# One written order for every engine, and PSUM banks shared in four pairs, in an attention and feed-forward kernel

## The chip, the cores and the metric

The kernel runs on one core of a Trainium2 chip. The time is device microseconds (us) of one execution; the number that is compared is the median of several runs. TensorE is called PE, its weight loads PEld, VectorE DVE, ScalarE ACT, GpSimd POOL and SyncE SP, as in the profile.

## What is computed

```python
# q, k, v: (4, 8, 768, 64); n_sink = 4; window = 128
scores = q @ k.T / 8
keep   = (key < 4) | ((0 <= query - key) & (query - key < 128))
a      = softmax(where(keep, scores, -1e9))
x      = (a @ v) with the heads side by side        # (3072, 512)
h      = (x @ w1) * (x @ w2)                        # 1024 wide
out    = (h @ w3) @ w_out                           # (3072, 512)
```

## The kernel before

The work is cut into named units, and each unit has stages on different engines. A unit's first number is mostly the batch b (0 to 3).

- `c`: a weight that SP has loaded raw is cast to bf16, on ACT or DVE. `t3.i.h` (line 588) transposes half of row block i of w3 on PE and copies it out of PSUM; `fm.i.h` (line 618) multiplies it by w_out, two matmuls in each unit, so that `w3 @ w_out` becomes one folded weight `w3o`.
- `tpk.b.kb` (line 295) transposes a block of keys and queries on PE; `td.b.kb` (line 303) does the same for later blocks by a DMA that SP issues. `ko`, `vo`, `sk` and `sv` are small DVE copies that bring sink keys and values beside the window's.
- `sc.b.x.t` are scores (lines 377, 428, 450): PE matmuls that use 64 rows of the array, ACT's exponential, DVE's product with a mask. `ss` are the scores of the sink keys, on 32 rows (line 348). `av.b.x.t` (lines 412, 483, 520) multiplies by the values; DVE then takes a reciprocal and scales.
- `xt` transposes the result on PE, `xd` by a DMA of SP (line 558).
- `g.b.c.dt.half` (line 571) is PE work for one chunk of tokens and one block of w1 (half 0, copied out by ACT at line 578) or w2 (half 1, multiplied by DVE at line 575).
- `p.b.m` (line 632) multiplies by `w3o`; ACT or DVE copies the result out (line 636) and SP stores it (line 641).

PE's order is a written list, `TURNS`. ACT, DVE and SP have no written order: a planner, `plan`, walks through time with a cost for each stage, estimated landing times of the loads (`landings`) and a table of small preferences (`LEAN`), and emits each engine's instructions in the order that results. So every engine's order is fixed when the program is built. Where PE would idle early on, the planner puts in matmuls on zeros (`keep_busy`, line 649).

PSUM has eight banks. The pool `ps_mm` has four one-bank buffers that rotate, for everything but scores; `ps_sc` has two buffers of two banks each, for scores and for the folds 0 to 3.

POOL issues the loads of q, k, v, of w1 and w2 and of part of w3, one after another. For batches 2 and 3 it waits, before each load, until the load four places back has landed (`send_load`).

Of the kernel before, what the change touches and what calls it, by code (L numbers as in the profile page):

```python
# [20 lines left out]
def kernel(  # L22
# [13 lines left out]
    nc = tc.nc  # L36
# [26 lines left out]
    PAIRED = ()  # L63
    BLOCKS = ((0, 0), (0, 1))
    SINKS = (1,)
    PAIRS = (2, 3)
    X_TURNED = ((1, 1), (1, 2)) + tuple((b, u) for b in (2, 3) for u in range(NT))
    HALVED = ((3, 1), (3, 2), (3, 3))
    SPLIT = 6
    OTHER = {("fm", 1, 3), ("fm", 7, 3), ("p", 2, 2), ("p", 2, 3), ("p", 2, 5), ("p", 3, 1), ("p", 3, 2), ("p", 3, 4),  # L70
             ("t3", 0, 1), ("t3", 1, 1), ("t3", 2, 1), ("t3", 3, 1), ("t3", 5, 0), ("t3", 6, 1), ("t3", 7, 1), ("tpk",
             0, 1), ("tpk", 1, 1), ("xt", 0, 0, 0), ("xt", 0, 2, 0), ("xt", 0, 2, 2), ("xt", 1, 0, 0)}
# [5 lines left out]
    work = ctx.enter_context(tc.tile_pool(name="work", bufs=3))  # L78
# [46 lines left out]
    AHEAD = 4  # L125
    sent = []

    def send_load(b, dst, src):

        if b >= 2 and len(sent) >= AHEAD:  # L130
            nc.gpsimd.tensor_copy(spent[:], sent[-AHEAD])  # L131
        nc.gpsimd.dma_start(out=dst, in_=src)  # L132
        sent.append(dst[:, 0, 0:1])

    def of_pair(b, m):

        x = kqN[b][:, 2 * m:2 * m + 2].rearrange("p k i x -> p (k i x)")
        return x.rearrange("p (i h s d) -> p i h s d", i=2, s=2, d=D)

    def load_qk(b, kb):  # L140

        if (b, kb // 2) in PAIRED:
            for i, src in enumerate((k, q)):
                if kb % 2 == 0:
                    send_load(b, of_pair(b, kb // 2)[:, i].rearrange("p h s d -> p h (s d)"),
                              src[b, :, kb * P:kb * P + 256, :].rearrange("h (p s) d -> p h (s d)", s=2))
            return
        for src, dst in ((k, kN), (q, qN)):
            send_load(b, heads(dst[b][:, kb, :]), rows(src, b, kb * P, (kb + 1) * P))

    def load_v(b, kb):

        for s in VSLOTS[kb] if b in LATE else (kb,):
            t0, t1 = KEYS[s] if b in LATE else (kb * P, (kb + 1) * P)
            send_load(b, vN[b][:, s, :, 0:D], rows(v, b, t0, t1))
# [48 lines left out]

    nudge = {}
# [77 lines left out]
    def copy_stage(name, act, act_us, dve_us):  # L283

        return ("act", act_us) if act != (name in OTHER) else ("dve", dve_us)

    def transposes(b, kb):

        tp = ps_mm.tile([P, 2, NP, P], BF16, tag="mm", name="tp")
        m, s = kb // 2, kb % 2  # L290
        paired = (b, m) in PAIRED
        for i, src in enumerate((kN[b], qN[b])):
            for r in range(NP):
                turn = of_pair(b, m)[:, i, 2 * r:2 * r + 2, s, :] if paired else src[:, kb, r * P:(r + 1) * P]
                nc.tensor.transpose(tp[:, i, r, :], turn, ident)  # L295
        yield
        copier(("tpk", b, kb), False)(kqT[b][:, :, :, bass.ds(256 * m + s, P, step=2) if paired else slice(kb * P, (kb + 1) * P)],
                              tp[:])
        yield
# [43 lines left out]
    def sink_scores(b, t0, t1):  # L343

        sp = ps_mm.tile([P, (t1 - t0) * 256], FP32, tag="mm", name="sp")
# [14 lines left out]
    def late_scores(b, r, u):  # L360
# [12 lines left out]
        sc = ps_sc.tile([P, 2, 512], FP32, tag="sc", name="sc")  # L373
# [5 lines left out]
        ex = work.tile([P, 2, 512], BF16, tag="ex", name="ex")  # L379
        nc.scalar.activation(ex[:, :, 0:n], sc[:, :, 0:n], ACTF.Exp, scale=scale)  # L380
        yield
        am = work.tile([P, 2, 512], BF16, tag="am", bufs=4, name="am")
        mv = 2 * min(u, 1)
        nc.vector.tensor_mul(am[:, :, 0:n], ex[:, :, 0:n], maskt[:, mv:mv + 1, 0:n].to_broadcast([P, 2, n]))  # L384
        ams[b, r, u] = am
        yield

    def late_values(b, r, u):
# [3 lines left out]
        av = ps_mm.tile([P, n, 2, D + 1], FP32, tag="mm", name="av")  # L392
# [18 lines left out]
        for x, (o, lhs, rhs) in enumerate(todo):  # L411
            nc.tensor.matmul(o, lhs, rhs, start=(x == 0), stop=(x == len(todo) - 1), skip_group_check=True)  # L412
        yield
        m = P if u == 0 else 112
        rec = work.tile([P, 3, 2, 1], FP32, tag="rec", name="rec")
        nc.vector.reciprocal(rec[0:m, 0:n], av[0:m, :, :, D:D + 1])  # L416
        if (b, u) not in xns:
            xns[b, u] = work.tile([P, n, NP, 2, D], BF16, tag="xn" if u else "xa", bufs=3 if u else 1, name="xn")
# [3 lines left out]
    def scores(b, r, t):  # L422
        c0 = P if t == 0 else 0
        sc = ps_sc.tile([P, 2, 512], FP32, tag="sc", name="sc")
# [7 lines left out]
        ex = work.tile([P, 2, 512], BF16, tag="ex", name="ex")  # L432
        nc.scalar.activation(ex[:, :, c0:], sc[:, :, c0:], ACTF.Exp, scale=scale)
        yield
        am = work.tile([P, 2, 512], BF16, tag="am", bufs=4, name="am")
        m0 = MA if t == 0 else MT
        mk = maskt[:].rearrange("p (o v) x -> p o (v x)", o=1)[:, :, m0:m0 + 512 - c0].to_broadcast([P, 2, 512 - c0])
        nc.vector.tensor_mul(am[:, :, c0:], ex[:, :, c0:], mk)
        ams[b, r, t] = am
        yield  # L440

    def block_scores(b, j, r0, r1):

        kbs = [kb for kb in (j - 1, j) if kb >= 0]
        sc = ps_sc.tile([P, 2, r1 - r0, len(kbs), P], FP32, tag="sc", name="sc")
        for r in range(r0, r1):
            for s, kb in enumerate(kbs):
                for e in range(2):
# [4 lines left out]
        ex = work.tile([P, 2, 512], BF16, tag="ex", name="ex")  # L453
        nc.scalar.activation(ex[:], sc[:].rearrange("p e r s q -> p e (r s q)"), ACTF.Exp, scale=scale)
        yield
        am = work.tile([P, 2, 512], BF16, tag="am", bufs=4, name="am")
# [4 lines left out]
                             .to_broadcast([P, 2 * (r1 - r0), n]))  # L461
        for r in range(r0, r1):
# [3 lines left out]
    xns = {}  # L466

    def block_values(b, j, r0):

        t, i = j // 2, j % 2  # L470
        av = ps_mm.tile([P, 2, 2, D + 1], FP32, tag="mm", name="av")
# [10 lines left out]
        for n, (o, lhs, rhs) in enumerate(todo):  # L482
            nc.tensor.matmul(o, lhs, rhs, start=(n == 0), stop=(n == len(todo) - 1),
                             skip_group_check=True)
        yield
        rec = work.tile([P, 3, 2, 1], FP32, tag="rec", name="rec")[:, 0:2]
        nc.vector.reciprocal(rec, av[:, :, :, D:D + 1])
        if (b, t) not in xns:
            xns[b, t] = work.tile([P, 2, NP, 2, D], BF16, tag="xn", bufs=3, name="xn")
# [4 lines left out]
    def block_x_transposes(b, j):  # L494

        t, i = j // 2, j % 2
        xt = ps_mm.tile([P, NP, P], BF16, tag="mm", name="xt")
        for r in range(NP):
            nc.tensor.transpose(xt[:, r, :], xns[b, t][:, i, r, :, :].rearrange("p e d -> p (e d)"), ident)
        yield  # L500
# [3 lines left out]
    def values(b, r, t):  # L504

        am = ams.pop((b, r, t))
        av = ps_mm.tile([P, 2, 2, D + 1], FP32, tag="mm", name="av")
# [11 lines left out]
        for n, (o, lhs, rhs) in enumerate(todo):  # L519
            nc.tensor.matmul(o, lhs, rhs, start=(n == 0), stop=(n == len(todo) - 1),  # L520
                             skip_group_check=True)
        yield
        rec = work.tile([P, 3, 2, 1], FP32, tag="rec", name="rec")[:, 0:2]
        nc.vector.reciprocal(rec, av[:, :, :, D:D + 1])
        if (b, t) not in xns:
            xns[b, t] = work.tile([P, 2, NP, 2, D], BF16, tag="xn", bufs=3, name="xn")
# [4 lines left out]
    def x_transposes(b, r0, t):  # L531

        xt = ps_mm.tile([P, 2, 2, P], BF16, tag="mm", name="xt")
        for r in range(2):
            for i in range(2):
                nc.tensor.transpose(xt[:, r, i, :],
                                    xns[b, t][:, i, r0 + r, :, :].rearrange("p e d -> p (e d)"),
                                    ident)
        yield
# [4 lines left out]
    def late_x_transposes(b, u, i):  # L544
# [3 lines left out]
        xt = ps_mm.tile([P, NP, m], BF16, tag="mm", name="xt")  # L548
        for r in range(NP):
            nc.tensor.transpose(xt[:, r, :], xns[b, u][0:m, i, r, :, :].rearrange("p e d -> p (e d)"), ident[0:m, 0:m])  # L550
        yield
# [3 lines left out]
    def x_transposes_dma(b, t, i):  # L555
# [3 lines left out]
                                    in_=xns[b, t][0:q1 - q0, i].rearrange("p r e d -> p (r e d)"))  # L559
        yield  # L560
# [3 lines left out]
    def gate(b, c, dt, half):  # L564
# [4 lines left out]
        pg = ps_mm.tile([P, n], FP32, tag="mm", name="pg")  # L569
# [4 lines left out]
        if half:  # L574
            nc.vector.tensor_mul(ab[b][:, dt, tk], gate_a.pop((b, c, dt))[:], pg[:])  # L575
        else:
            a_sb = work.tile([P, n], FP32, tag="a_sb", bufs=4, name="a_sb")
            nc.scalar.copy(a_sb[:], pg[:])  # L578
# [5 lines left out]
    def fold_w3(i, j0, j1):  # L584

        tp = ps_mm.tile([P, j1 - j0, P], BF16, tag="mm", name="tp3")
# [17 lines left out]
    def folded(i):  # L604
        return ("fm", i, len(FM[i]) - 1)

    def fold_mm(i, j0, j1):

        if i >= 4:
            if j0 == 0:  # L610
                held[i] = ps_mm.tile([P, DM], FP32, tag="mm", name="pw")
            po = held[i][:]
        else:
            if i % 2 == 0 and j0 == 0:
                held[i // 2] = ps_sc.tile([P, 2, DM], FP32, tag="sc", name="ph")
# [12 lines left out]
    def project(b, m, n0, n1):  # L628

        po = ps_mm.tile([P, n1 - n0], FP32, tag="mm", name="po")  # L630
# [14 lines left out]
    def keep_busy(n):  # L645

        pz = ps_mm.tile([P, 512], FP32, tag="mm", name="pz")
# [4 lines left out]
    arrive = {}  # L652
    arrive["vc",] = 20.0

    def service(what, *i):
        if what == "qkv":
            return [(0.95 if i[0] == 0 else 0.87, (1.65 if (i[0], s // 2) in PAIRED and x != "v" else 1) * (0.845 if i[0] == 0 else 0.9 if i[0] == 1 else 1.72),
                     [(x, i[0], n) for n in ((s, s + 1) if (i[0], s // 2) in PAIRED and x != "v" else (s,))])
                    for y, kb in pieces(*i)
                    for x, s in ([("k", kb), ("q", kb)] if y == "kq" else  # L660
                                 [("v", s) for s in (VSLOTS[kb] if i[0] in LATE else (kb,))])
                    if (i[0], kb // 2) not in PAIRED or x == "v" or kb % 2 == 0]
        if what == "w3":
            return [(0.75, 1.3 * (i[1] - i[0]), [("w3", x) for x in range(*i)])]
        if what == "wo":
            return [(0.81, 0.65 * (i[1] - i[0]), [("wo", x) for x in range(*i)])]
        return [(0.8, 1.34 * (i[1] - i[0]), [(w,) + (n,) for n in range(i[0], i[1])]) for w in ("w1", "w2")]
# [536 lines left out]
```

## Time and profile before

| | |
|---|---|
| median of 3 runs | 192.89 us (192.27 to 193.19) |
| the profiled execution | 193.17 us, of which its span is 191.5 us |
| PE busy | 184.6 us, 96% of the span |
| DVE, ACT, POOL busy | 125.9, 102.5, 91.5 us |
| PE matmuls at line 571 (gates) and 632 (projection) | 91.5 and 43.0 us busy |
| moved by DMA | 30.02 MB |

A row of the timeline gives start and length in us, engine, line, operation, what is written and read, and how many instructions were merged; in brackets stands the idle time before it with what ended it. Matmuls overlap, so the step between the starts of rows tells what a matmul costs, and its own length tells how long its result takes. In a row of the stretches the numbers behind the stretch are its length and the busy us (with the count of instructions) of PE, PEld, DVE, ACT and POOL. A row of a group ends with busy us, mean ns of one, and the idle us before them. Some records of matmuls are missing from the trace.

### The profile page before, as it was taken

How to read it: one execution, taken by the hardware profiler on the slowest of the kernel's cores; microseconds unless marked ns; L12 is line 12 of the kernel's file. 1: busy time of each engine (PE TensorE's matmuls, PEld its weight loads, DVE VectorE, ACT ScalarE, POOL GpSimd, SP SyncE). 2: the span in 40 equal slices, each digit the busy share in tenths (PEclk: the TensorE clock that was granted, in tenths of full speed). 3: DMA queues.
4: the chain of work that ended last, by engine and by line, in shares of the span. 5: the costliest groups of instructions: out<-in, count | busy, mean ns of one | idle time of the engine just before them, and what ended most of it. 6: DMA issues, size and time to landing. Idle time of an engine off the chain costs nothing.

```text
span 191.5 us, 4799 instructions
## 1 busy us (share of the span) xinstructions
PE 184.6 (96%) x1874; PEld 122.3 (64%) x1893; DVE 125.9 (66%) x302; ACT 102.5 (54%) x171; POOL 91.5 (48%) x149
## 2 busy tenths in 40 slices
PE   7899999999999999999999999999999999999993
PEld 2345557988688776767788876665556675555442
DVE  4554688846688778878896877785888653532320
ACT  3363578643967568756738575464687233230112
POOL 4298977699992468786756667640000000000000
PEclk9999999999999999999999999999999999999999
DMA  6999999999999999999999999999511022000525
GB/s 217 407 377 171 170 159 197 195 163 153 150 179 177 125 188 154 153 144 226 180 180 220 182 160 158 185 181 190 193 29 39 13 67 88 6 0 14 184 94 205
DMA packets 112551, 30.02 MB, mean 157 GB/s; under 512 B 103184, under 2 KB 108432, under 8 KB 112528
## 3 DMA queue, kind: packets, MB, share of 16 engines
q0 software_dynamic: 82640, 12.72, 97.7%
q1 hardware_dynamic: 29744, 16.92, 37.7%
q8 instruction: 15, 0.25, 0.5%
q10 hardware_dynamic: 144, 0.07, 0.1%
q14 instruction: 8, 0.07, 0.1%
HBM read 30.15 MB, written 6.29 MB: 190 GB/s over the span
## 4 chain that ended last, share of the span: by engine, by line
PE 76%; DMA 13%; POOL 6%; issue 1%; SPq 1%; ACT 0%
PE pg L571 42%; PE po L632 21%; DMA w_sb<-in_moe_w_dram 5%; PE av L412 5%; PE sc L377 5%; DMA vN<-in_v_dram 4%; DMA ab<-in_moe_w_out_dram 4%; POOL w_sb L159 3%; POOL kqN L132 2%; PE tp L295 1%; SPq L217 1%; PE av L520 1%; PE sc L428 1%; POOL vN L132 0%; ACT w_sb L636 0%
## 5 line engine op out<-in xcount | busy, mean ns | idle before, releaser
L571 PE MATMUL pg<-xT,w_sb 128*128 128x256 bf16 (+3 forms) x640 | 91.5, 294 | 0.2 <-DMA w_sb<-in_moe_w_dram 0.2
L571 PEld LDWEIGHTS <-w_sb 128*128 128x128 bf16 x640 | 59.4, 98 | 20.7 <-DMA w_sb<-in_moe_w_dram 0.4
L578 ACT COPY a_sb<-pg 128x256 f32<-128x256 f32 (+3 forms) x80 | 32.6, 417 | 34.1 <-PE pg L571 31.9
L575 DVE TENSOR_TENSOR ab<-a_sb,pg 128x256 bf16<-128x256 f32 (+3 forms) x80 | 37.1, 471 | 19.4 <-PE pg L571 18.1
L632 PE MATMUL po<-w3o,ab 128*128 128x512 bf16 (+2 forms) x193 | 43.0, 361 | 0.7
L380 ACT ACTIVATE ex<-sc 128x928 bf16<-128x928 f32 (+1 forms) x36 | 34.4, 972 | 5.0 <-PE sc L377 4.7
L632 PEld LDWEIGHTS <-ab 128*128 128x128 bf16 x208 | 19.3, 98 | 19.3
L636 ACT COPY w_sb<-po 128x512 f32<-128x512 f32 (+2 forms) x19 | 10.6, 558 | 29.9 <-PE po L632 28.1
L132 POOL DMA_DIRECT2D vN<-in_v_dram x27 | 24.2, 905 | 3.4 <-issue 1.8
L384 DVE TENSOR_TENSOR am<-ex,maskt 128x928 bf16<-128x928 bf16 (+1 forms) x36 | 23.1, 651 | 1.2 <-ACT ex L380 1.1
L132 POOL DMA_DIRECT2D kqN<-in_q_dram x24 | 21.8, 909 | 3.9 <-issue 2.8
L132 POOL DMA_DIRECT2D kqN<-in_k_dram x24 | 21.9, 911 | 3.5 <-issue 2.2
L419 DVE TENSOR_TENSOR xn<-av,rec 112x256 bf16<-112x256 f32 (+1 forms) x36 | 16.9, 469 | 1.2
L412 PEld LDWEIGHTS <-am 128*128 128x128 bf16 x312 | 12.9, 98 | 4.0
L416 DVE RECIPROCAL rec<-av 112x4 f32<-112x4 f32 (+1 forms) x36 | 6.6, 183 | 10.9 <-PE av L412 10.6
L412 PE MATMUL av<-vN,am 128*128 128x65 bf16 x216 | 13.7, 193 | 0.0
L636 DVE COPY w_sb<-po 128x512 f32<-128x512 f32 (+1 forms) x7 | 4.3, 633 | 10.5 <-PE po L632 7.3
L131 POOL CAST spent<-kqN 128x1 f32<-128x1 bf16 x24 | 6.3, 264 | 9.5 <-DMA kqN<-in_k_dram 7.1
L377 PE MATMUL sc<-kqT 64*128 64x112 bf16 (+3 forms) x168 | 10.0, 218 | 0.0
L618 PE MATMUL ph<-wo_sb,kown 128*128 128x512 bf16 x31 | 8.5, 380 | 0.7 <-DVE wo_sb L598 0.3
L377 PEld LDWEIGHTS <-kqT 64*128 64x128 bf16 x168 | 6.8, 94 | 3.5 <-issue 3.0
L377 PE MATMUL sc<-kqT,kown 64*128 64x112 bf16 (+2 forms) x120 | 8.7, 208 | 0.0
(94 smaller groups left out, 178.4 us busy)
## 6 DMA issues: line engine op xcount, KB each, us to landing
out_dram<-w_sb SPq DMA_DIRECT2D x20, 256.0 KB
vN<-in_v_dram POOLq DMA_DIRECT2D x27, 128.0 KB, 6.5
kqN<-in_k_dram POOLq DMA_DIRECT2D x24, 128.0 KB, 6.1
kqN<-in_q_dram POOLq DMA_DIRECT2D x24, 128.0 KB, 6.1
w_sb<-in_moe_w_dram POOLq DMA_DIRECT2D x9, 256.0 KB, 8.3
ab<-in_moe_w_dram SPq DMA_DIRECT2D x4, 512.0 KB
ab<-in_moe_w_out_dram SPq DMA_DIRECT2D x2, 512.0 KB
kqN<-in_moe_w_out_dram SPq DMA_DIRECT2D x2, 512.0 KB
```

Source lines behind the costliest of these rows:

```text
L132: nc.gpsimd.dma_start(out=dst, in_=src)
L377: nc.tensor.matmul(sc[:, e, c:c + m], keys[hp], qT[b][hp, r, q0:q0 + m], start=True, stop=True)
L380: nc.scalar.activation(ex[:, :, 0:n], sc[:, :, 0:n], ACTF.Exp, scale=scale)
L384: nc.vector.tensor_mul(am[:, :, 0:n], ex[:, :, 0:n], maskt[:, mv:mv + 1, 0:n].to_broadcast([P, 2, n]))
L412: nc.tensor.matmul(o, lhs, rhs, start=(x == 0), stop=(x == len(todo) - 1), skip_group_check=True)
L419: nc.vector.tensor_mul(xns[b, u][0:m, 0:n, r, :, :], av[0:m, :, :, 0:D], rec[0:m, 0:n].to_broadcast([m, n, 2, D]))
L571: nc.tensor.matmul(pg[:], w_sb[:, kk, dt * P:(dt + 1) * P], xT[b][:, kk, tk], start=(kk == 0), stop=(kk == NP - 1))
L575: nc.vector.tensor_mul(ab[b][:, dt, tk], gate_a.pop((b, c, dt))[:], pg[:])
L578: nc.scalar.copy(a_sb[:], pg[:])
L618: nc.tensor.matmul(po, w3T[i][:, j, :], wo_sb[:, j, :], start=(j == 0), stop=(j == KFF - 1))
L632: nc.tensor.matmul(po[:], ab[b][:, kk, m * P:(m + 1) * P], w3o[:, kk, n0:n1], start=(kk == 0), stop=(kk == KFF - 1))
L636: copier(("p", b, m) + ((n0,) if n0 else ()), n0 != DM // 2)(o_sb, po[:])
```

## The change

Four PSUM tiles of two banks take the place of both pools. Every use of PSUM takes its bank (`room`) or its pair of banks (`wide`) from a written string, `PLACES`, so scores may stand in any pair, and anything else in any free bank. The buffers in SBUF are handed out by the same written order: masked scores get six buffers where there were four, the reciprocals one where there were three.

The planner, its landing times, its costs, `TURNS` and `LEAN` go. One list, `ORDER`, names a unit each time one of its stages is issued; the first mention is its first stage. So PE's order and those of ACT, DVE and SP are all read from one list. In it, units of scores stand up to three in a row (in two places with a unit of sink scores beside them), where they stood one or two. Four entries `fill` put in 14 matmuls on zeros, where there were 17. The set `OTHER` changes which of ACT and DVE makes a copy in some units. POOL's wait for the load four places back now begins at key block 3 of batch 1.

```diff
-    ps_sc = ctx.enter_context(tc.tile_pool(name="ps_sc", bufs=2, space=PSUM))
-    ps_mm = ctx.enter_context(tc.tile_pool(name="ps_mm", bufs=4, space=PSUM))
+    psum = ctx.enter_context(tc.tile_pool(name="psum", bufs=1, space=PSUM))
+    PLACES = (
+        "4457067516754576765476754013401234546701267067452735015730257056746546745764576451034523675206745676"
...
+    places = iter(int(x) for x in PLACES)
+    pairs = [psum.tile([P, 2, 512], FP32, tag=f"pair{i}", name=f"pair{i}") for i in range(4)]
+    def room(*shape, dtype=FP32):
+        n = next(places)
+        x = pairs[n // 2][:, n % 2]
...
+    def wide(*shape):
+        x = pairs[next(places)][:]
...
+    ex_slots = Slots("ex", 3, [P, 2, 512], BF16)
+    am_slots = Slots("am", 6, [P, 2, 512], BF16)
+    a_slots = Slots("a_sb", 4, [P, 448], FP32)
...
+    rec_slots = Slots("rec", 1, [P, 3, 2, 1], FP32)
...
-    AHEAD = 4
+    AHEAD, PACED = 4, (1, 3)
...
-        if b >= 2 and len(sent) >= AHEAD:
+        if (b, kb) >= PACED and len(sent) >= AHEAD:
             nc.gpsimd.tensor_copy(spent[:], sent[-AHEAD])
...
-        sc = ps_sc.tile([P, 2, 512], FP32, tag="sc", name="sc")
+        sc = wide(P, 2, 512)
...
-        pg = ps_mm.tile([P, n], FP32, tag="mm", name="pg")
+        pg = room(P, n)
...
-    def plan(emit):
...
-    landings()
-    plan(True)
...
+    ORDER = """
+        c.w3.0.0 c.wo.0.0 fill.11 t3.0.1 t3.0.1 t3.0.0 t3.0.0 fill.1 fm.0.0 c.w3.2.0 t3.2.0 t3.2.0 t3.2.1 t3.2.1
+        fill.1 fm.2.0 c.w3.4.0 t3.4.1 t3.4.0 c.wo.2.512 c.wo.2.0 fill.1 fm.0.1 fm.2.1 t3.4.1 t3.4.0 fm.4.0
+        c.w3.1.0 fm.4.1 t3.1.0 t3.1.0 t3.1.1 fm.1.0 fm.1.1 c.wo.4.0 fm.4.2 c.wo.6.0 fm.4.3 fm.4.3 fm.2.2 fm.2.3
+        t3.1.1 c.w3.3.0 t3.3.0 t3.3.0 t3.3.1 fm.0.2 fm.0.3 fm.1.2 fm.1.3 fm.1.3 t3.7.0 fm.3.0 fm.3.1 t3.3.1
...
+        sc.1.1.1 sc.1.1.1 sc.1.1.1 sc.1.3.1 sc.1.0.1 sc.1.0.1 g.1.0.6.1 g.1.0.6.1 g.1.0.2.1 g.1.0.2.1 td.2.1
+        td.2.0 g.1.0.4.1 g.1.0.4.1 sc.1.3.1 sc.1.3.1 sc.1.0.1 g.1.0.7.0 g.1.0.7.0 av.1.1.1 av.1.1.1 sc.1.2.1
...
+        g.3.1.1.1 g.3.1.0.1 g.3.1.0.0 g.3.1.0.1 p.2.4 p.2.2 p.2.2 p.2.2 g.3.1.5.1 p.3.5.256 p.3.5.256 p.3.5.256
+        p.3.0 p.3.2 p.3.2 p.3.2 p.3.3 p.3.3 p.3.3 p.3.4 p.3.4 p.3.4 p.3.5 p.3.5 p.3.5.384 p.3.5.384 p.3.5.384
+        p.3.5
+    """
+    running = {}
+    for entry in ORDER.split():
...
+            if entry not in running:
+                running[entry] = JOBS[what](*of)
+            next(running[entry])
```

In the excerpt the banks for `sc.1.1.1`, `sc.1.3.1` and `sc.1.0.1` are 0 and 1, 2 and 3, 6 and 7; the gates behind them, `g.1.0.6.1`, `g.1.0.2.1`, `g.1.0.4.1` and `g.1.0.7.0`, take 4, 5, 0 and 6.

More of the change, by code (lines that the diff above doesn't have):

```diff
@@ L466, with x_done @@
     xns = {}
+    turned, read = collections.Counter(), collections.Counter()
+    def x_done(b, t, of):
+        turned[b, t] += 1
+        if turned[b, t] == of:
+            (xa_slots if b in LATE and t == 0 else xn_slots).give((b, t))
     def block_values(b, j, r0):
         t, i = j // 2, j % 2
-        av = ps_mm.tile([P, 2, 2, D + 1], FP32, tag="mm", name="av")
+        av = room(P, 2, 2, D + 1)
         todo = []
@@ L574, in gate @@
         if half:
-            nc.vector.tensor_mul(ab[b][:, dt, tk], gate_a.pop((b, c, dt))[:], pg[:])
-        else:
-            a_sb = work.tile([P, n], FP32, tag="a_sb", bufs=4, name="a_sb")
-            nc.scalar.copy(a_sb[:], pg[:])
+            nc.vector.tensor_mul(ab[b][:, dt, tk], gate_a.pop((b, c, dt)), pg)
+            a_slots.give((b, c, dt))
+        else:
+            a_sb = a_slots.take((b, c, dt))[:, 0:n]
+            nc.scalar.copy(a_sb, pg)
             gate_a[b, c, dt] = a_sb
@@ L610, in fold_mm @@
             if j0 == 0:
-                held[i] = ps_mm.tile([P, DM], FP32, tag="mm", name="pw")
+                held[i] = room(P, DM)
             po = held[i][:]
@@ L645, in keep_busy @@
     def keep_busy(n):
-        pz = ps_mm.tile([P, 512], FP32, tag="mm", name="pz")
+        pz = room(P, 512)
         for _ in range(n):
             nc.tensor.matmul(pz[:], idle[:, 0:P], idle, start=True, stop=True)
[L652 to L667, printed above, removed]
@@ L669, in landings @@
-    def landings(RAW=2.0, POOL=3.0, DGE=1.3, RAMP=(0.75, 1.0)):
-        queues = {"sp": [(RAW, 1.28, 1.0 if n < 2 else 1.9, [("raw",) + x[:3]]) for n, x in enumerate(raws)],
-                  "pool": [(gen, us, 1.8, keys) for x in order for gen, us, keys in service(*x)]}
-        left = {n: [us for _, us, _, _ in q] for n, q in queues.items()}
-        at = {n: 0 for n in queues}
-        landed, issue, ready, now = [], POOL, [], 0.0
-        while any(at[n] < len(q) for n, q in queues.items()):
-            while len(ready) < len(queues["pool"]) and (len(ready) < 8 or len(landed) > len(ready) - 8) \
-                    and at["sp"] >= hold:
-                if not ready and hold:
-                    issue = max(issue, arrive[("raw",) + raws[hold - 1][:3]] + 0.3)
-                if len(ready) >= 8:
-                    issue = max(issue, landed[len(ready) - 8])
-                issue += queues["pool"][len(ready)][0]
-                ready.append(max(5.8, issue + DGE))
-            busy = [n for n, q in queues.items() if at[n] < len(q)
-                    and now >= (q[at[n]][0] if n != "pool" else ready[at[n]] if at[n] < len(ready) else 1e9)]
-            small = queues["pool"][at["pool"]][3][0][0] if "pool" in busy else ""
-            for n in busy:
-                i = int(now - RAW) if now >= RAW else 0
-                share = 1.0 if len(busy) == 1 else 0.5 if small not in "kqv" else 0.79 if n == "sp" else 0.13
-                left[n][at[n]] -= 0.02 * share * (RAMP[i] if i < len(RAMP) else 1.0)
-                if left[n][at[n]] <= 0.0:
-                    lag, keys = queues[n][at[n]][2:]
-                    for key in keys:
-                        arrive[key] = now + lag + min(1.5, max(0.0, 0.25 * (now - 36.0)))
-                    if n == "pool":
-                        landed.append(now + lag)
-                    at[n] += 1
-            now += 0.02
@@ L701 @@
-    tasks = {}
-    SP_US = 0.7
-    def task(name, prio, gen, stages, after=(), loads=(), ring=None, started=(),
-             half=False, slots=1, paced=False):
-        tasks[name] = dict(name=name, prio=prio + nudge.get(name, 0.0), gen=gen, stages=stages, after=list(after),
-                           loads=list(loads), ring=ring, started=list(started), half=half,
-                           slots=slots, paced=paced)
-    made = {}
-    for n, ((what, i0, i1, e), (dst, src)) in enumerate(zip(raws, casts)):
-        cuts = ((0, 1024, e),) if e in ("act", "dve") else ((0, 512, "dve"), (512, 1024, "act"))
-        for c0, c1, eng in cuts:
-            name = ("c", what, i0, c0)
-            us = (c1 - c0) / 1024
-            task(name, n, cast(eng == "act", dst[:, c0:c1], src[:, c0:c1]),
-                 [(eng, 0.16 + 0.88 * us if eng == "act" else 0.07 + 0.62 * us)], loads=[("raw", what, i0, i1)])
-            for x in range(c0 // 512, c1 // 512):
-                made[(what, i0, x) if what == "w3" else (what, i0 + x, 0)] = name
@@ L1168, with cast_of, scores_of @@
-    landings()
-    plan(True)
+    def cast_of(what, i0, c0):
+        n = [x[:2] for x in raws].index((what, i0))
+        e, (dst, src) = raws[n][3], casts[n]
+        c1 = c0 + 512 if e == "both" else 1024
+        return cast(e == "act" or (e == "both" and c0 > 0), dst[:, c0:c1], src[:, c0:c1])
+    def scores_of(b, x, t):
+        if b in LATE:
+            return late_scores(b, x, t)
+        if (b, t) in BLOCKS:
+            return block_scores(b, *PARTS[t][x])
+        return scores(b, x, t)
@@ L1172 @@
+    """
+    running = {}
+    for entry in ORDER.split():
+        what, *of = entry.split(".")
+        of = [int(x) if x.lstrip("-").isdigit() else x for x in of]
+        if what == "fill":
+            keep_busy(*of)
+        elif what == "loads":
+            for x in order:
+                if x[0] == "qkv" and x[1] > 0:
+                    load(*x)
+        else:
+            if entry not in running:
+                running[entry] = JOBS[what](*of)
+            next(running[entry])
 _INS = ['q', 'k', 'v', 'n_sink', 'window', 'moe_w1', 'moe_w2', 'moe_w3', 'moe_w_out']
```

483 lines of the change are left out of this document (159 added, 324 removed), and 158 rows, old and new, of tables (LEAN, TURNS).

## The prediction

> **What bounds the kernel now.** I read the page's busy times and its chain first, then PE's waits, then the busy times of the stretches, then PE's timeline where the work changes kind.
>
> ```profile
> PE 184.6 (96%) x1874; PEld 122.3 (64%) x1893; DVE 125.9 (66%) x302; ACT 102.5 (54%) x171; POOL 91.5 (48%) x149
> PE 76%; DMA 13%; POOL 6%; issue 1%; SPq 1%; ACT 0%
> ...
> PE pz L649 <- DVE ksbd L226: 1.3, 1, 1.3
> PE ph L618 <- DVE wo_sb L598: 0.3, 1, 0.3
> PE ph L618 <- DVE kown L593: 0.3, 1, 0.3
> PE tp L588 <- DVE w_sb L598: 0.2, 1, 0.2
> PE pw L618 <- issue: 0.2, 1, 0.2
> PE pg L571 <- DMA w_sb<-in_moe_w_dram: 0.2, 1, 0.2
> ```
>
> PE is busy for 96% of the span and holds 76% of the chain; the rest of the chain (DMA, POOL) lies in the loads at the start. The six rows are all the waits that PE itself shows: 2.5 us, four of them in the folds of the weights, one for the first zeros, and one for the last slice of w1 or w2. None is for an ACT or DVE instruction that empties PSUM behind the folds. So PSUM is not what PE waits for, and a change of banks alone gives back nothing.
>
> ```profile
> 17.40:45.70 28.30, 27.88 (x337) 20.91 (x339) 20.37 (x48) 18.23 (x31) 23.00 (x33) 1.00 2.00 173
> 45.70:188.30 142.60, 141.68 (x1463) 94.84 (x1475) 96.80 (x239) 77.06 (x133) 57.72 (x93) 1.00 1.30 135
> ...
> 17.38 1.21 PE L588 MATMUL tp<-ident,w_sb 128*128 128x128 bf16 x16
> 40.87 3.67 PE L571 MATMUL pg<-xT,w_sb 128*128 128x256 bf16 x32 [0.16 <-DMA w_sb<-in_moe_w_dram]
> 44.82 1.04 PE L571 MATMUL pg<-xT,w_sb 128*128 128x256 bf16 x8
> 45.70 0.61 PE L295 MATMUL tp<-ident,kqN 128*128 128x128 bf16 x8
> PEld L295 <- DMA kqN<-in_q_dram: 0.2, 1, 0.2
> 180.71 7.53 PE L632 MATMUL po<-w3o,ab 128*128 128x512 bf16 x43
> ```
>
> I cut the span at three places that both lists share. At 17.38 PE begins `t3.3.0`, the last block whose weights SP loads raw. At 45.70 it begins `tpk.0.5`, for the last keys and queries of batch 0; the row of PEld shows a transpose of keys and queries waiting for q's load, so I take 45.7 as about the earliest that `tpk.0.5` can be. At 188.24 (180.71 + 7.53) the last matmul ends; 3.2 us of copying and storing follow, and the new list ends with the same two units, so that tail stays. In the last 142.6 us PE's idle time is 0.92 us in all.
>
> **The change part by part.** *Runs of scores.* Scores use 64 rows of the array, sink scores 32, all else 128.
>
> ```profile
> 75.18 0.20 PE L412 MATMUL av<-vp,am 128*128 128x65 bf16 x1
> 75.22 0.19 PE L412 MATMUL av<-vN,am 128*128 128x65 bf16 x1
> 75.34 0.22 PE L377 MATMUL sc<-kqT 64*128 64x112 bf16 x2
> ...
> 75.65 0.21 PE L377 MATMUL sc<-kqT 64*128 64x112 bf16 x2
> 75.70 0.22 PE L377 MATMUL sc<-kqT,kown 64*128 64x128 bf16 x2
> 75.85 0.45 PE L571 MATMUL pg<-xT,w_sb 128*128 128x320 bf16 x2
> ...
> 58.14 0.19 PE L377 MATMUL sc<-kqT,kown 64*128 64x64 bf16 x2
> 58.16 0.36 PE L377 MATMUL sc<-kqT 64*128 64x256 bf16 x6
> ```
>
> Going in costs 0.12 us from start to start (75.22 to 75.34) against 0.03 to 0.04 within values: 0.09 extra. Going out costs 0.15 (75.70 to 75.85) against 0.05 within scores: 0.10 extra. Between two units of scores there is nothing extra (58.14 to 58.16). I call it a turn, 0.095 us. Counting kinds in `TURNS` gives 56 turns, in the first mentions in `ORDER` 42. Behind `tpk.0.5`, where PE is never idle for long, it is 43 against 35: 8 x 0.095 = 0.76 us, and that is on the path. The other six lie ahead of it, where loads set the pace, and count only in the next step.
>
> *What is done by 45.7.* Ahead of `tpk.0.5` the new list has eight gate units that came later before, and leaves for later six that came earlier: two more gate units of 256 tokens, each 0.44 us (the eight matmuls from 44.82 to 45.70 are two units). That is 0.88 us off the rest, if PE gets there in time. Can it? The raw weights come no faster than before:
>
> ```profile
> 9.99 0.62 ACT L598 CAST wo_sb<-ab 128x512 bf16<-128x512 f32 x1 [0.80 <-DMA ab<-in_moe_w_out_dram]
> 10.24 1.00 DVE L598 CAST wo_sb<-ab 128x512 bf16<-128x512 f32 x1
> 11.29 0.81 PE L618 MATMUL ph<-wo_sb,kown 128*128 128x512 bf16 x3 [0.30 <-DVE wo_sb L598]
> 12.58 0.61 PE L588 MATMUL tp<-ident,w_sb 128*128 128x128 bf16 x8
> 13.03 0.38 PE L649 MATMUL pz<-ksbd 128*128 128x512 bf16 x1
> 13.01 0.42 DVE L593 COPY kown<-tp 128x512 bf16<-128x512 bf16 x1 [1.44 <-PE tp L588]
> 13.49 1.90 PE L618 MATMUL ph<-wo_sb,kown 128*128 128x512 bf16 x8
> 15.22 0.59 PE L618 MATMUL pw<-wo_sb,kqN 128*128 128x512 bf16 x2
> 15.09 0.69 DVE L598 CAST w_sb<-kqT 128x1024 bf16<-128x1024 f32 x1 [0.35 <-DMA kqT<-in_moe_w_dram]
> ```
>
> A fold unit costs (15.22 - 13.49) / 4 = 0.43 us, a half transpose (13.03 - 12.58) / 2 = 0.225. In both lists PE waits near 11 us for the cast of w_out's rows 2 and 3 (before, DVE ends it at 11.24 and PE goes on at 11.29, a step of 0.05). In the new list DVE is free when the load lands, so the cast ends at 10.99, and `fm.0.1` starts at 11.04. Four fold units take PE to 12.77, two half transposes to 13.22; the copy of the first (matmul tail 0.16, step 0.05, copy 0.42, step 0.05 behind 12.99) is there at 13.67, so PE waits 0.45. Six fold units then end at 16.3, and the cast for `t3.3.0` (landed 15.09, behind two other DVE entries at 15.2 to 15.9) is ready. So `t3.3.0` begins at 16.3, where it began at 17.38: 1.1 us earlier, with three fold units (1.30 us) still to do. From there to `tpk.0.5` the new list has 1.30 + 0.88 - 6 x 0.095 = 1.61 us more work. Before, the stretch took 28.3 us with at least 0.42 of it idle. So 16.3 + 28.3 - 0.4 + 1.6 = 45.8. The ends: not below 45.65 (the landing), and 46.8 if the new list has another 1.0 us of load waits of its own (w1 and w2 land slice by slice until 40.87, and the list uses each soon after). I take 45.8, since the stretch before ran with so little idle.
>
> *Copies that change engine, zeros left out, buffers.* The first four half transposes of block 0 and 2 are copied by ACT; `fm.0.0` gets later by one copy of 0.6 us, hidden by the wait for the cast at 11. Three fewer zero matmuls fill idle time only. One reciprocal buffer costs nothing, as DVE alone writes and reads it. Six masked buffers bring nothing by themselves.
>
> *POOL's wait.*
>
> ```profile
> L131 POOL CAST spent<-kqN 128x1 f32<-128x1 bf16 x24 | 6.3, 264 | 9.5 <-DMA kqN<-in_k_dram 7.1 <-DMA kqN<-in_q_dram 2.3
> ```
>
> Nine loads of batch 1 (a key and a query load for each of three blocks, and three of values) get such a copy, 9 x 0.26 = 2.4 us, and wait for a landing. Behind them on POOL stand the loads of batches 2 and 3, and behind these, on SP, the transposes `td`. The first user of the last of those loads is `td.1.5` for `sc.1.0.2`, which the list puts 32 us of PE work behind `tpk.0.5`, at 78. Cost nothing; without that cover each us late is a us of PE. Stores and `xd` transposes move along SP's queue too; the last, `xd.3.2.0`, stands nine units of PE work (9 us) ahead of its gate. Nothing.
>
> *New waits.* No row shows them, so bounds: 0 from below (the old order had almost none; a gain of the 0.92 us idle at most), and from above one ACT entry at each of the nine groups of three or four units behind 45.7, 2.1 us by the rival below. I take 0.2, near the old order's rows, as all engines are in order in both.
>
> **Sum.** 45.8 + (142.6 - 0.88 - 0.76) + 0.2 = 186.96 for the end of the last matmul, against 188.24: 1.3 us less. The profiled execution took 193.17 us (span 191.5 and 1.7 around it), 0.28 above the median of 192.89. So 192.89 - 1.3 = 191.6 us.
>
> In the Trainium skill, "Perfetto Trace Analysis", section "Matmul Optimizations", asks that all eight PSUM banks be used. By that advice pooling the banks would bring a gain of its own. The kernel before has all eight in use already (four and two pairs), and PE's waits above show no bank wait, so by the rows the sum gets nothing from it.
>
> **Rivals.** *The start gains nothing.* If the new list loses more than it wins between 17 and 46 us, `tpk.0.5` comes at 46.8: then the end is 1.0 later, and 192.6 us remain. For it: the list uses slices of w1 and w2 as they land, and four waits of PE in the folds are of that kind. Against it: 1.1 us of lead at `t3.3.0`.
>
> *Six of eight banks hold scores.* Three units leave one pair for all else until ACT has read a unit.
>
> ```profile
> L380 ACT ACTIVATE ex<-sc 128x928 bf16<-128x928 f32 x24 | 22.3, 945 | 2.5 <-PE sc L377 2.3
> 77.15 0.43 ACT L578 COPY a_sb<-pg 128x320 f32<-128x320 f32 x1 [0.45 <-PE pg L571]
> 77.47 0.95 ACT L380 ACTIVATE ex<-sc 128x928 bf16<-128x928 f32 x1
> ```
>
> Take `sc.1.1.1`, `sc.1.3.1`, `sc.1.0.1`, from t = 0 on PE, 0.21 each. ACT reads the first from 0.42 (0.21, tail 0.16, step 0.05) to 1.36; the next exponential of the list, of `sc.1.0.1`, starts 0.84 later (an ACT entry hands on 0.11 before its end: 77.15 + 0.43 against 77.47) and ends at 2.20. PE starts gates of 320 tokens (0.44 x 320 / 256 = 0.55) at 0.72: two in the free pair, the third at 1.82 in bank 0 (free at 1.42), the fourth at 2.37 in bank 6 (free at 2.26). It fits by 0.11. If ACT is one copy late (0.32), PE loses 0.21 there, over nine groups 1.9 to 2.1 us, and the kernel ends at 193.6. If it is two copies late, 0.53 x 9 = 4.8 us, and 196.3: slower. It decides from (1.3 + 0.96) / 9 = 0.25 us a group. For it: the margin of 0.11 is small, and one engine out of step hands it on to all. Against it: ACT is busy 54% only.
>
> The Trainium skill says in "TensorEngine Tiling (Array Packing)", section "Gotcha 1: PSUM Pressure", that row tiling makes PSUM scarcer, because row tiles write to different banks. That rule speaks against longer runs of scores; before, at most two pairs were held, and no row here shows three, so it adds no number, and the two prices above stand.
>
> *The runs bring nothing*, because a turn is hidden: excluded by the steps of start to start above.
>
> **How the numbers follow.** What a measurement of this kernel can tell from no change is about 0.5%, 0.96 us. Forecast, 191.6 (its own range 190.4 to 192.0): 0.62. The start gains nothing, 192.6: 0.20. Scores hold the banks, two copies late, 196.3, or from 193.9 on: 0.15. Something near one copy late, 193.6: 0.03. The low end takes `tpk.0.5` at 45.65 and the old 0.92 us of idle and my 0.2 gone: 191.6 - 0.15 - 0.92 - 0.2 = 190.3; the high end is 193.6, and about 0.17 lies outside. Faster: 0.62, with a little of it below the bound lost and a little of the second case gained. Within: 0.21. Slower: 0.17.
>
> **What would show it.** `t3.3.0` (third block of line 588's transposes, from the end of the fold's first twelve units) at 16.3; `tpk.0.5` at 45.8; from there to the last matmul 141 us; scores in runs of three with a step of 0.02 between units, and no new row among PE's waits above 0.3 us. PE waiting for ACT or DVE at gates behind a run of scores would make it wrong by the second rival, PE waiting for loads between 17 and 46 by the first.

## The result, and the profile of the changed kernel

The changed kernel takes 278.26 us (median; 277.37 to 279.96) against 193.04 us before: a ratio of 1.440, 95% interval 1.427 to 1.453. The forecast was 191.6 us. The sign was wrong, and the size lies far outside the range. Medians in this document are of all runs; the ratios and their intervals leave out runs that took over 1.5% longer than the fastest of the same kernel.

The page of the changed kernel, busy times first, then PE's row of the 40 slices and the granted clock:

```profile
PE 203.2 (73%) x1890; PEld 125.0 (45%) x1890; DVE 125.3 (45%) x298; ACT 104.8 (38%) x175; POOL 88.9 (32%) x158
...
PE   7787778667667477758596768798598777868774
...
PEclk9999979999999999999889989999999999999999
```

DVE and ACT do the same work as before (125.3 and 104.8 us against 125.9 and 102.5). PE is busy for 73% of the span where it was 96%, and no stage stands out: nearly every slice, from the first fold to the last output, lies between 5 and 8 tenths. Something that every unit meets costs time, not one late load. PE's own waits name it (line waited for, total, times, longest, us):

```profile
PE pair L615 <- DVE ab L619: 12.0, 14, 1.7
PE pair L615 <- ACT a_sb L623: 10.5, 18, 1.0
PE pair L674 <- ACT w_sb L678: 6.0, 6, 3.0
PE pair L674 <- DVE xn L442: 4.1, 3, 2.1
```

Line 615 is the gates' matmul, 674 that of the output; 619, 623 and 678 are the instructions that empty PSUM behind them, and 442 is the scaling that empties it behind the values. All rows of this list come to 70 us in 87 waits. Before, PE's waits were 2.5 us in six, and none was of this kind. The span is 85.6 us longer: 67.0 us of that are stops of PE (277.1 - 203.2 against 191.5 - 184.6), and 18.6 us are longer busy time, which was not taken apart. The last microseconds, where there is no other work, show one such wait after another (start, duration, engine, line, tiles; in brackets the idle time ahead and what ended it):

```profile
266.27 0.58 ACT L678 COPY w_sb<-pair 128x512 f32<-128x512 f32 x1 [3.08 <-PE pair L674]
266.91 1.89 PE L674 MATMUL pair<-w3o,ab 128*128 128x512 bf16 x8 [0.67 <-ACT w_sb L678]
...
268.83 0.58 ACT L678 COPY w_sb<-pair 128x512 f32<-128x512 f32 x1 [1.98 <-PE pair L674]
269.47 1.89 PE L674 MATMUL pair<-w3o,ab 128*128 128x512 bf16 x8 [0.67 <-ACT w_sb L678]
...
271.44 0.58 ACT L678 COPY w_sb<-pair 128x512 f32<-128x512 f32 x1 [2.02 <-PE pair L674]
272.07 1.03 PE L674 MATMUL pair<-w3o,ab 128*128 128x256 bf16 x8 [0.72 <-ACT w_sb L678]
```

The units here are `p.3.2`, `p.3.3`, `p.3.4`, `p.3.5`, and the list of banks gives them 5, 4, 5, 4. The copy of bank 5 ends at 266.85, and `p.3.3`, which writes bank 4, starts at 266.91. It waits 0.67 us for the reader of a bank that it doesn't touch: banks 4 and 5 are the halves of one tile, `pair2`. Before, 43 matmuls of the same kind stood back to back from 180.71 to 188.24.

So the theory to be tested (A in the expectations): a tile of two banks is one thing to the waits that are drawn between instructions. A matmul waits until whatever else used the tile earlier in program order has been read, and a copy waits until the neighbour has been written, or has been read by the other engine. The rivals: the written order has no slack, so that any small delay goes through all engines (B); runs of three scores hold six of the eight banks (C, the prediction's second rival).

### The profile page after: what moved, and what is told of

Its sections match the earlier page's. It is cut to its first block, busy times and chain, and to the rows that moved or that the text cites. A ratio compares the mean times of both kernels' runs of the same rounds, so it can differ in the third digit from the quotient of the medians.

```text
span 277.1 us, 4823 instructions
## 1 busy us (share of the span) xinstructions
PE 203.2 (73%) x1890; PEld 125.0 (45%) x1890; DVE 125.3 (45%) x298; ACT 104.8 (38%) x175; POOL 88.9 (32%) x158
## 5 line engine op out<-in xcount | busy, mean ns | idle before, releaser
L615 PE MATMUL pair<-xT,w_sb 128*128 128x256 bf16 (+3 forms) x640 | 96.6, 293 | 31.6 <-DVE ab L619 12.0
L623 ACT COPY a_sb<-pair 128x256 f32<-128x256 f32 (+3 forms) x80 | 32.1, 416 | 74.4 <-PE pair L615 65.6
L619 DVE TENSOR_TENSOR ab<-a_sb,pair 128x256 bf16<-128x256 f32 (+3 forms) x80 | 37.0, 471 | 50.2 <-PE pair L615 27.9
L674 PE MATMUL pair<-w3o,ab 128*128 128x512 bf16 (+2 forms) x208 | 47.3, 377 | 13.6 <-ACT w_sb L678 6.0
L400 ACT ACTIVATE ex<-pair 128x928 bf16<-128x928 f32 (+1 forms) x36 | 33.4, 971 | 20.5 <-PE pair L397 20.5
L678 ACT COPY w_sb<-pair 128x512 f32<-128x512 f32 (+2 forms) x20 | 11.1, 561 | 48.7 <-PE pair L674 48.0
L433 PE MATMUL pair<-vN,am 128*128 128x65 bf16 x216 | 13.6, 196 | 0.9 <-ACT a_sb L623 0.5
L660 PE MATMUL pair<-wo_sb,kown 128*128 128x512 bf16 x48 | 12.2, 379 | 1.4 <-ACT kqT L318 0.7
L442 DVE TENSOR_TENSOR xn<-pair,rec 112x256 bf16<-112x256 f32 x24 | 10.2, 424 | 0.8
L397 PE MATMUL pair<-kqT 64*128 64x112 bf16 (+3 forms) x168 | 9.8, 221 | 0.1
```

The costliest lines, as they stand in the source:

```text
L397: nc.tensor.matmul(sc[:, e, c:c + m], keys[hp], qT[b][hp, r, q0:q0 + m], start=True, stop=True)
L442: nc.vector.tensor_mul(xns[b, u][0:m, 0:n, r, :, :], av[0:m, :, :, 0:D], rec[0:m, 0:n].to_broadcast([m, n, 2, D]))
L615: nc.tensor.matmul(pg[:], w_sb[:, kk, dt * P:(dt + 1) * P], xT[b][:, kk, tk], start=(kk == 0), stop=(kk == NP - 1))
L623: nc.scalar.copy(a_sb, pg)
L660: nc.tensor.matmul(po, w3T[i][:, j, :], wo_sb[:, j, :], start=(j == 0), stop=(j == KFF - 1))
L674: nc.tensor.matmul(po[:], ab[b][:, kk, m * P:(m + 1) * P], w3o[:, kk, n0:n1], start=(kk == 0), stop=(kk == KFF - 1))
```

## The experiments

Each version is compared with the kernel before, run again beside it; that kernel's median was then 194.1 to 194.3 us.

**One tile for each bank.** The order and the list of banks stay; the tiles are single banks.

```diff
-    pairs = [psum.tile([P, 2, 512], FP32, tag=f"pair{i}", name=f"pair{i}") for i in range(4)]
+    banks = [psum.tile([P, 512], FP32, tag=f"bank{i}", name=f"bank{i}") for i in range(8)]
...
-        nc.scalar.activation(ex[:, :, 0:n], sc[:, :, 0:n], ACTF.Exp, scale=scale)
+        for e in range(2):
+            nc.scalar.activation(ex[:, e, 0:n], sc[e][:, 0:n], ACTF.Exp, scale=scale)
```

> The changed kernel with its order and its list of banks kept, but PSUM taken as eight tiles of one bank instead of four of two; what used both banks in one instruction (36 exponentials of scores, 12 block and first-batch ones, two copies of the fold) is done as two instructions of one bank each. Theory A (a pair is one thing to the program's waits: a matmul for one bank waits until the other bank has been read, and a copy waits until the other bank has been written): the waits of PE for DVE and ACT on the lines of the gates and of the output product (12.0, 10.5 and 6.0 us after) go under 3 us in all, PE is busy over 95 % of the span, and the time is 192 to 200 us; the forecast's 191.6 plus what some 50 more ACT instructions cost. Theory B (the written order itself has no slack, whatever the tiles): 260 us or more, the same rows of waits. Theory C (six of eight banks hold scores and the gates behind a run wait for copies): PE's waits remain behind runs of score units only, time 196 to 205 us.

Measured: 193.70 us, ratio to before 0.9992 (0.9963 to 1.0021). Its busy times, then its largest waits of PE:

```profile
PE 184.8 (97%) x1890; PEld 123.1 (64%) x1890; DVE 123.3 (64%) x300; ACT 105.0 (55%) x222; POOL 91.3 (48%) x158
```

```profile
PE bank L695 <- DVE ksbd L254: 1.3, 1, 1.3
PE bank L663 <- ACT kown L641: 1.0, 2, 0.7
```

The 85 us are gone with the tiles, though the order, the banks and the engines of the copies are the changed kernel's. The waits on the gates' and the output's lines are gone too; 2.8 us are left, all but 0.2 of it in the zeros and the folds. Theory B is out.

**The same pairs, with the waits between neighbours taken out.** This leaves every instruction as it is in the changed kernel.

```diff
+            for j, r, w in units[n ^ 1][-200:]:        # what touched the other bank
+                if i.engine != j.engine and not (w & (me[0] | me[1]) or r & me[1]):
+                    tc.declare_no_dep(i, j, reason="the other bank of a pair")
```

> The changed kernel with the same instructions in the same order on the same banks; only the waits between an instruction on one bank and one on the other bank of its pair are taken out where the two share no other data. Theory A: within 2 us of the forecast, 189.5 to 193.5 us, and at the tail the output products stand back to back (0.1 us or less between units, 0.67 us after). Theory B: 260 us or more. Theory C: 194 to 200 us with PE waits behind runs of scores.

Measured: 196.34 us, ratio 1.0137 (1.0103 to 1.0171): 82 of the 85 us, and outside the 189.5 to 193.5 that I gave. At the tail 56 output products stand back to back, from 183.06 to 191.90. The rest stood in and between the folds: `tpk.0.5` comes at 50.47, and from there to the last matmul it takes 141.4 us, as in the fifth run below (this kernel records every operation in one helper, line 98, so the tiles tell what is what):

```profile
25.03 0.61 PE L98 MATMUL pair<-ident,kqN 128*128 128x128 bf16 x8 [0.67 <-ACT w3o L98]
...
33.77 0.61 PE L98 MATMUL pair<-ident,kqN 128*128 128x128 bf16 x8 [0.67 <-ACT w3o L98]
```

Transposes of keys wait 0.67 us for a copy of the folded weight. A fold unit `fm.4` to `fm.7` holds its bank over four steps, and my edit knew the bank only in the first. The fifth run mends that.

**The kernel before, with false neighbours.** The reverse: the old order, and its four rotating banks first as four fixed tiles (control), then as the halves of two.

```diff
+    mms = [ps_mm.tile([P, 512], FP32, tag=f"mm{i}", name=f"mm{i}") for i in range(4)]           # control
+    mms = [ps_mm.tile([P, 2, 512], FP32, tag=f"mm{i}", name=f"mm{i}") for i in range(2)]        # pairs
```

> The kernel before with the four banks of its rotating pool as four fixed tiles of one bank, given out by the plan's own record of which is free first. A control for the next run: every theory expects the time before, 193.0 us within 1 us.

> The kernel before, same order, with the same four banks as the halves of two two-bank tiles; the score tiles are as before. Theory A: every unit of gates, values, transposes and outputs waits for its neighbour's eviction, at 0.3 to 0.6 us for each of some 230 units, so 240 to 300 us, with rows of PE waiting for ACT and DVE on the gates' line of 8 us or more each. Theories B and C: 193 us within 1 us, like the control.

Measured: the control 194.68 us (ratio 1.0033, 0.9999 to 1.0067), the pairs 221.22 us (1.1434, 1.1384 to 1.1483). The busy times, then PE's largest waits of the run with pairs:

```profile
PE 195.6 (89%) x1893; PEld 124.1 (57%) x1893; DVE 125.8 (57%) x302; ACT 101.7 (46%) x171; POOL 91.8 (42%) x149
```

```profile
PE mm L581 <- DVE ab L585: 3.3, 8, 0.6
PE mm L581 <- ACT w_sb L646: 1.9, 4, 0.6
```

The old order loses 26.5 us to nothing but the grouping of four banks into two tiles. The mean clock was 0.999, so a lower clock has no part in it. The mechanism is A's; the size is not what I gave (240 to 300 us), and the two rows of waits are 3.3 and 1.9 us, not 8. A single wait costs about what I said: PE's list has 43 waits of 17.6 us in all, 0.4 us each, where before it has six of 2.5 us. But only about one unit in seven shows one (I had counted 230 units; the lists have some 270 that use these banks). Another 11 us are in PE's busy time, 195.6 us against 184.6. My price had each unit wait for the whole of its neighbour's copy; that it is mostly past by then is what I take from it, and no run shows it by itself.

**All banks parted.** As the second run, with the folds' later steps included.

```diff
                 home[entry] = at[0]
+                if what == "fm" and of[0] >= 4 and of[1]:
+                    home[entry] = home[f"fm.{of[0]}.0"]
```

> As the second run, and now the folds of the weights that hold one bank over four steps are parted from the other bank too; the second run left those in, and its 1.5 us above the first run's span are lost ahead of 35 us, in the folds. So every instruction is the changed kernel's own and only waits for a bank's true users are left: the written order by itself. If the order is worth what the forecast says: 190.5 to 192.0 us. If the first run's time was the order's and not the price of its split exponentials: 192.5 to 194.0 us, no difference from before within 0.5 %. If runs of three scores hold the banks: above 194 us, with PE waits behind them.

Measured: 193.52 us, ratio 1.0012 (0.9972 to 1.0052). This is the written order alone, with the changed kernel's own instructions in its own banks: no difference from before, and not the forecast's 190.5 to 192.0 either. So the loss lay in the waits that the program draws, not in the banks. No run tells the matmuls' waits from the copies'. (The spans of the second and the first run are 194.9 and 191.4 us, so 3.5 us apart, not the 1.5 of the expectation.) Its stretches, cut at the prediction's places (`t3.3.0`, `tpk.0.5`, the last matmul):

```profile
16.54:47.41 30.87, 29.61 (x352) 22.69 (x353) 20.60 (x47) 18.39 (x33) 25.34 (x37) 1.00 1.98 171
47.41:188.94 141.53, 140.44 (x1459) 94.09 (x1467) 95.63 (x237) 75.72 (x131) 56.91 (x101) 1.00 1.34 135
```

**Thirty-five other numbers.** The changed kernel with its pairs, its waits and its order; only the last 35 digits of the list of banks differ.

```diff
-        "2672634576107451034567230617236147175104756107674523572467540135014051034501230675275647541075642352"
-        "567467467467365476546754545")
+        "2672634576107451034567230617236147175104756107674523572467540135014051034501230675275647541064720340"
+        "144624624624752014262462046")
```

> The changed kernel with its four two-bank tiles and its order; only the last 35 numbers of the list of banks are others, those behind the last score: each unit takes a pair that was last read at least four entries of the list ago where there is one. In the changed kernel these 35 units take 61 us from the last score's matmul to the last matmul (213.3 to 274.2), against 33.6 us in the run with one-bank tiles. Theory A (a unit waits for the other bank's reader): most of the 27 us comes back, 250 to 258 us in all. Theory B (the order has no slack): 278 us within 2 us, since every instruction stands where it stood and each bank's own last reader is no nearer than before.

Measured: 265.75 us, ratio 1.3737 (1.3654 to 1.3820), so 12.5 us less than the changed kernel. That is not the 250 to 258 us that I gave, and the fault was in my reading: I had taken the scores at 213.3 for the last ones, and the last stand at 225.93. First the stretch of the changed kernel from there to its last matmul (bounds, length, PE busy, the other engines, clock, DMA), then this run over the same units, then PE's timeline of this run there:

```profile
226.15:274.17 48.02, 35.98 (x208) 17.33 (x208) 10.37 (x23) 11.36 (x20) 0.00 (x0) 1.00 0.21 66
```

```profile
227.07:261.47 34.40, 33.57 (x205) 17.53 (x208) 10.14 (x23) 11.22 (x20) 0.00 (x0) 1.00 0.27 85
```

```profile
236.96 3.61 PE L674 MATMUL pair<-w3o,ab 128*128 128x512 bf16 x15 [0.67 <-ACT w_sb L678]
240.41 12.27 PE L615 MATMUL pair<-xT,w_sb 128*128 128x448 bf16 x64
252.64 8.83 PE L674 MATMUL pair<-w3o,ab 128*128 128x512 bf16 x55
```

The 35 units need 34.40 us instead of 48.02, as in the run with one-bank tiles (155.00 to 188.39, 33.4 us), and 64 and 55 matmuls stand without a gap. All but 1.0 us of the loss in this stretch goes away when most neighbours in time are put into different tiles. Of what is left, 0.67 us is a true wait: the new numbers give `p.3.0` bank 4, which `p.3.1` has just used. And `p.2.3` and `p.2.1`, in banks 0 and 1 of one tile, follow each other without a stop; in the list the matmuls of both stand ahead of both copies, so there is no earlier reader to wait for.

**The first batch by single banks.** A try at joining the early part of the first run with the late part of the fifth: the fifth run's kernel, with the first batch's exponentials and the two paired copies of folds split.

```diff
-        scalar_.activation(ex[:, :, c0:], sc[:, :, c0:], ACTF.Exp, scale=scale)
+        for e in range(2):
+            scalar_.activation(ex[:, e, c0:], sc[:, e, c0:], ACTF.Exp, scale=scale)
```

> The fifth run's kernel (pairs as tiles, banks parted), with the exponentials of the first batch and the two copies of folds done bank by bank as in the first run, the later exponentials whole. In the first run the second-last keys' transpose of batch 0 (`tpk.0.5`) stood at 46.2 us and 142.2 us followed to the last matmul; in the fifth it stood at 47.4 and 141.5 followed. If both parts add up, the last matmul ends at 46.2 + 141.5 = 187.7, against 188.2 before: 0.5 us under the kernel before, 192.3 to 193.8 us, no difference that can be told within 0.5 %. If the earlier start of the first run was only the spread of when loads land, the last matmul ends at 188.5 to 189.5 us and the time is that of the fifth run.

Measured: 193.45 us, ratio 1.0000 (0.9968 to 1.0032). `t3.3.0` stands at 17.28, `tpk.0.5` at 47.67, and the last matmul ends at 189.30, 141.6 us later. The late stretch repeats the fifth run's, the early one doesn't repeat the first's. DVE's cast of w_out's rows 2 and 3, which starts as their load lands, shows why (first, fifth and seventh run):

```profile
9.46 0.43 DVE L646 CAST wo_sb<-ab 128x512 bf16<-128x512 f32 x1 [0.57 <-DMA ab<-in_moe_w_out_dram]
10.34 0.43 DVE L98 CAST wo_sb<-ab 128x512 bf16<-128x512 f32 x1 [0.59 <-DMA ab<-in_moe_w_out_dram]
11.09 0.43 DVE L98 CAST wo_sb<-ab 128x512 bf16<-128x512 f32 x1 [0.57 <-DMA ab<-in_moe_w_out_dram]
```

In the three, `t3.3.0` stands at 15.80, 16.54 and 17.28, so 6.2 to 6.3 us behind the cast's start each time, and the first run's lead there was the spread of the loads between executions. No version here beats the kernel before by more than can be told.

## Why the prediction was wrong, point by point

*The step that failed* is "New waits. No row shows them, so bounds: 0 from below", with 2.1 us as the upper end and 0.2 taken. It measured 85 us. The bound was built from ACT entries behind runs of scores, so from banks that are truly in use. The worked example gives four gates "banks 4, 5, 0 and 6" and lets each wait for its own bank alone. But the change also makes tiles of two banks that are shared by two units at a time, and that is no property of a bank. In the kernel before, no tile holds two results that are emptied apart, so its trace has no row from which to price this; the diff shows it in the one line that makes the pairs. It had to be a rival, with its place (every unit), its price (one copy and two steps, some 0.67 us, where the neighbour was just used) and no upper end near 2 us.

*"So PSUM is not what PE waits for, and a change of banks alone gives back nothing."* Right for the gain: with neighbours parted, pooled banks bring nothing (1.0012). Taken as leave to price the change of banks at nothing, it was wrong. The Trainium skill's advice in "Perfetto Trace Analysis", section "Matmul Optimizations", to use all eight banks gave no gain here either: both kernels use all eight, one at 193 us and one at 278.

*Six of eight banks hold scores.* The forecast held that it fits. In the fifth run the longest stop of PE directly behind a run of scores, and its longest stop behind 50 us, are

```profile
92.54 1.24 PE L98 MATMUL pair<-w3o,ab 128*128 128x512 bf16 x5 [0.16 <-issue]
...
119.25 0.57 PE L98 MATMUL pair<-xT,w_sb 128*128 128x320 bf16 x3 [0.22 <-DVE xn L98]
```

so 0.16 us behind one run, and 0.22 us between two gates; the rival had 0.21 or 0.53 us at each of nine groups. The Trainium skill's rule in "TensorEngine Tiling (Array Packing)", section "Gotcha 1: PSUM Pressure", cost no more than that here.

*Turns and moved gates.* From `tpk.0.5` to the last matmul the forecast had 142.6 - 0.88 - 0.76 + 0.2 = 141.16 us. The fifth run took 141.53, and the seventh 141.6. So the sum of these terms held within 0.4 us; no run measures them one by one, and PE's idle time there was 1.09 us, where it had been 0.92. (The first run took 142.2, with its exponentials split.) The trace gives the sink scores as 128*32, so all 128 rows and 32 columns of the array, not 32 rows; without a kind of their own the turns would be 42 and 34, still eight apart.

*What is done by 45.7.* `t3.3.0` came at 16.54 (forecast 16.3), `tpk.0.5` at 47.41 (45.8). PE had 29.61 us of work between them, which is the 29.5 that I had summed; but it also stood still for 1.26 us, which I had taken to be nothing "since the stretch before ran with so little idle". The first rival, "the start gains nothing", was right in this, at 1.6 us rather than 1.0, but not by the slices of w1 and w2 that it named. Below are PE's two largest stops there, the start of `tpk.0.5` and, last, a row of the kernel before:

```profile
25.74 0.40 PE L98 MATMUL pair<-ident,w_sb 128*128 128x128 bf16 x4 [0.37 <-DMA w_sb<-in_moe_w_dram]
...
40.09 0.38 PE L98 MATMUL pair<-ident,xn 128*128 128x128 bf16 x4 [0.49 <-DVE xn L98]
...
47.41 0.61 PE L98 MATMUL pair<-ident,kqN 128*128 128x128 bf16 x8
...
19.90 0.23 PEld L295 LDWEIGHTS <-kqN 128*128 128x128 bf16 x4 [0.17 <-DMA kqN<-in_q_dram]
```

One wait is of `t3.5.0`, for the block of w3 that POOL loads, one of `xt.0.2.1`, for a result that the new list asks for too early. The lead at `t3.3.0` itself was real. It stands 6.2 us behind the landing of w_out's rows 2 and 3 (10.34 to 16.54), where the old order needs 7.4 us (9.99 to 17.38 in the kernel before, 9.43 to 16.82 in the control). It was lost again on the way to `tpk.0.5`. The lower end, "not below 45.65 (the landing)", rested on a misreading: PEld's wait for q's load stands at 19.90, not at 45.7, and in the control above the old order has `tpk.0.5` at 44.94. So even without the pairs the forecast of 191.6 us was too good: 0.24 + 1.37 + 0.37 us at the three cuts turn the forecast's 186.96 for the last matmul into 188.94.

*Copies, zeros, buffers and POOL's wait* were priced at nothing. In the fifth run PE shows no wait above 0.2 us for a transposing DMA, and the whole order comes out even; the parts were not tried one by one.

## What to carry to other kernels

Count the users of a tile, not of a bank: when two units that run at the same time share one tile, every instruction of one may wait for the other, even where they touch different banks, and here a busy row of PE that fell evenly over the whole span was its mark. If an order rests on banks being independent, give each bank a tile of its own (splitting the few instructions that read two cost no time that could be measured here, with ACT busy for 55% of the span), or put units that follow each other into different tiles. And where a change makes a kind of sharing that the old trace never had, the old trace gives no upper bound for it: it belongs among the rivals.

## What the runs showed of the hardware

The granted clock of PE fell by half for some microseconds behind some of its stops. Stretches of the changed kernel (bounds, length, PE busy, the other engines, granted clock, DMA share, GB/s), and PE's starts beside them:

```profile
34.00:36.00 2.00, 1.83 (x5) 0.70 (x5) 0.71 (x2) 0.28 (x1) 1.27 (x2) 0.56 1.45 196
92.00:94.00 2.00, 1.03 (x8) 0.78 (x8) 0.52 (x1) 0.73 (x3) 2.00 (x4) 1.00 1.13 72
138.00:140.00 2.00, 2.00 (x21) 1.20 (x19) 0.24 (x2) 0.58 (x1) 0.00 (x0) 0.50 0.69 22
150.00:152.00 2.00, 1.95 (x21) 1.86 (x20) 1.28 (x4) 0.95 (x4) 0.00 (x0) 1.00 0.79 244
164.00:166.00 2.00, 1.68 (x5) 0.58 (x5) 0.27 (x1) 0.00 (x0) 0.00 (x0) 0.50 0.00 0
```

```profile
34.17 3.54 PE L660 MATMUL pair<-wo_sb,kqN 128*128 128x512 bf16 x8 [1.75 <-DVE xn L527]
...
92.57 1.03 PE L615 MATMUL pair<-xT,w_sb 128*128 128x256 bf16 x8 [1.98 <-DVE xa L442]
...
136.08 3.06 PE L674 MATMUL pair<-w3o,ab 128*128 128x512 bf16 x8 [3.04 <-ACT w_sb L678]
...
148.70 3.51 PE L615 MATMUL pair<-xT,w_sb 128*128 128x224 bf16 x32 [1.55 <-DVE ab L619]
...
164.32 3.37 PE L674 MATMUL pair<-w3o,ab 128*128 128x512 bf16 x8 [2.06 <-DVE xn L442]
```

Behind stops of 1.75, 3.04 and 2.06 us the clock was 0.56, 0.50 and 0.50, and eight matmuls of 512 columns took 3.54, 3.06 and 3.37 us, against 1.89 for eight in the tail above; behind stops of 1.55 and 1.98 us it was 1.00. So the length of one stop alone doesn't decide it, and no run here shows what else does. The Trainium skill says in "TensorE: Matmul & The Clock Gate", section "HAM oscillation — how this bites in real kernels", that idle gaps of PE should stay under about 3.4 us; here the clock fell behind three shorter ones, so the measurement decides. This made the loss somewhat larger (the mean clock was 0.981), but didn't make it: in the run with the 35 other numbers the mean clock was lower, 0.974, and the time shorter.
